# Two more pairs of heads turned on VectorE and through memory instead of by TensorE, in a banded attention with a gated product

## The chip, the core and the metric

The kernel runs on one core of a Trainium2 chip. TensorE (PE) multiplies matrices, VectorE (DVE), ScalarE (ACT) and GpSimd (POOL) work on vectors, and SyncE (SP) issues the transfers between the chip's memory and the on-chip tiles. The metric is the device time of one execution in microseconds. Three runs of the kernel before took 724.47, 725.68 and 729.17 us; the median is 725.68.

## What is computed

The reference is a local attention with global tokens, followed by a gated product of dense layers:

```
k_all, v_all = concat([k_g, k_l]), concat([v_g, v_l])
out_g = softmax(q_g @ k_all.T / 8) @ v_all               # 32 global tokens see everything
s_ll  = where(|i - j| <= 32, q_l @ k_l.T / 8, -1e9)      # 512 local tokens see a band
s_lg  = q_l @ k_g.T / 8                                  # and the global tokens
out_l = softmax(concat([s_lg, s_ll])) @ concat([v_g, v_l])
x     = rows of concat([out_g, out_l])                   # 4608 tokens, 512 wide
out   = ((x @ w1) * (x @ w2)) @ w3 @ w_out               # 1024 wide inside
```

There are 8 batches and 8 heads of width 64.

## The kernel before

**Attention.** Two heads of one batch make a *pair*; the 32 pairs are numbered from 0, four to a batch (`pair`, with `m` the number and `NP` = 4). For each pair TensorE makes the scores (`scores`, 32 instructions in the program, 64 records in the trace), VectorE takes each block's maximum (`minus_max`, eight times), ScalarE the exponentials (`exps`, eight times), and the probabilities have to be turned so that they can stand as weights of the product with the values (`values`). Its result is divided by the sums on VectorE (`normalize`) and has to be turned too, since the dense layers want a token in a column. It is then split into a high and a low part (`convert`, `xh` and `xl`).

**Two ways to turn.** With `m < TP` the probabilities are turned by TensorE: `transposes` makes four 128×128 transposes for each of the two heads into a PSUM bank, and `transposed` copies the bank to the tile `Pt` on ScalarE or VectorE. With `m >= TP`, `turn` turns 32×32 blocks on VectorE (one instruction, the step `tn`), `turned_out` (step `po`) issues four transfers to a tile `Pd` in memory that put the blocks in their places, and `turned_in` (step `pi`) one transfer back to `Pt`. The same holds for the tokens with `XT`: `back` makes four transposes by TensorE into the bank `b`, or `values_turn` (step `vn`), `values_out` (`vw`, four transfers to `vd`) and `values_in` (`vi`, one transfer to `xr`) go by VectorE and memory. Before, `TP` and `XT` are 4: pairs 0 to 3, which are batch 0, go by TensorE, the others by memory. `Pt` and the normalized tile `vo` have one buffer each, `Pd` and `vd` three.

**Weights.** The weights come as 64-bit numbers and are unpacked on ScalarE and VectorE (`fetch` and `unit`, from raw tiles that are used in turn). `w3 @ w_out` is multiplied out first on TensorE, in 64 products of 128×512 (`fold`, two records each), and split (`fold_split`).

**Dense layers.** The tokens are taken in twelve blocks `k`; block 0 holds three quarters of batch 0. For each `k` and each of eight column blocks `m`, `first` makes two products of twelve matmuls (`ap` and `bp`, three for each of the four pairs of the batch), `gate_a`, `gate_b`, `gate_hi` and `gate_lo` multiply and split them, and `second` multiplies with the product of `w3` and `w_out`. The first product of block 0 needs the tokens of pairs 0 to 3.

**The order.** Nothing is scheduled at run time. Every step has a number in the table `ORDER_OF`, and for some a letter that names its engine (A, D or P). `in_order` sorts all steps by these numbers, and they are written to the engines in that sequence, so that each engine's queue, SP's too, is in this order, and an instruction that waits holds up what stands behind it on its engine. `add` gives a step its engines and what it depends on, `take` and `read` what a buffer's reuse depends on.

Of the kernel before, what the change touches and what calls it, by code (L numbers as in the profile page):

```python
# [19 lines left out]
def i(ap):  # L20
# [8 lines left out]
LAG, TP, XT, LATE, VC, VL = 0, 4, 4, 4, 4, 10  # L29
# [15 lines left out]
    load="5 9 2 4 26 3 16 10 45 133 44 60 193 72 200 230 190 310 154 203 291 246 373 301 442 457 404 447 680  "  # L45
# [5 lines left out]
    clear="0 1 8",  # L51
    edges="27",
    warm="17",
    fetch="6 7 21 15 19 24 41 59 55 69 76 79 101 96 107 122 126 142 158 148 162 219 257 255 256 285 304 340 366  "
    "341 369 403 189 216 225 441 488 498 500 519 554 558 584 569 611 642 645 604",
    unit="D22 12 23 D25 29 33 A47 48 56 A42 30 49 A43 52 63 D57 53 64 D67 65 78 D85 91 99 D86 74 87 D100 103  "
# [8 lines left out]
    fold="50 70 81 117 119 141 170 175 58 71 93 118 123 140 167 197 62 94 97 116 127 139 204 209 82 90 98 115  "  # L65
    "145 153 159 164 215 226 234 262 267 283 299 325 270 279 307 332 380 397 413 418 317 324 337 393 398  "
    "439 445 462 345 348 354 360 386 407 423 435",
    w34h="D187 A220 D236 D169 A326 A444 D475 A438",
    w34l="198 250 260 171 338 449 479 455",
    vc="A13 A137 D173 P83 P46 D40 P199 A342 P252 P275 P298 D295 A432 D392 A683 A706 D704 A752 P796 A774 P895  "  # L70
# [4 lines left out]
    vs="P61 A66 P84 D160 A92 A73 P80 D228 A102 P95 P108 P112 A243 P263 D356 A269 P850 A854 D905 A878 D906  "  # L75
# [7 lines left out]
    kc="A11 D14 A20 P28 D77 P113 P106 A165 P224 D265 P306 D311 A472 P478 A516 A486 A634 D615 A649 D667 P764  "  # L83
# [4 lines left out]
    s="18 51 182 239 294 364 485 539 646 711 793 833 915 955 1057 1098 1152 1217 1302 1342 1431 1474 1569  "  # L88
    "1609 1699 1757 1858 1904 1983 2027 2109 2171",
    mm="37 32 34 36 31 38 35 39 178 88 68 149 131 146 105 161 210 227 191 192 195 194 196 212 245 248 259  "  # L90
# [11 lines left out]
    ex="155 111 75 54 130 166 89 134 211 128 180 168 179 152 156 184 237 244 221 214 202 201 233 218 288 253  "  # L102
# [11 lines left out]
    tp="174 181 223 238 251 276 329 344",  # L114
    pt="A176 D183 A229 A241 A264 A280 D330 A358",
    v="188 242 292 370 490 588 687 714 798 858 916 958 1058 1100 1157 1223 1305 1373 1433 1478 1571 1614  "
    "1703 1751 1860 1905 1985 2029 2112 2172 2260 2293",
    iv="172 231 274 346 469 518 625 700 735 822 887 935 982 1072 1106 1198 1249 1331 1383 1472 1561 1600  "
    "1691 1749 1815 1880 1928 2014 2051 2159 2206 2272",
    nm="222 258 343 411 514 596 693 723 807 860 926 963 1068 1103 1173 1235 1325 1376 1447 1492 1577 1623  "  # L120
    "1717 1754 1865 1912 1988 2039 2117 2178 2267 2296",
    xt="254 335 384 421",
# [990 lines left out]
```

## Time and profile before

| What | us |
|---|---|
| median of three runs | 725.68 |
| the profiled execution's own time | 725.34 |
| its span on the core | 723.4 |
| TensorE busy | 708.2 |
| VectorE busy | 452.4 |
| ScalarE busy | 346.5 |
| GpSimd busy | 143.4 |

The profile is of one execution. Busy times are unions of the engine's instructions. A matmul's end is modelled, and consecutive matmuls overlap in the records; the distance from start to start, which the chain of waits shows, is what one costs TensorE. The chain of waits follows the last instruction back to whatever released each step. The DMA share is the mean busy share of the core's 16 DMA engines.

### The profile page before, as it was taken

To read this page: it belongs to the slowest core of one execution; us is meant where nothing else is said; L and a number is where in the kernel's file an instruction comes from. 1 tells how busy PE (TensorE), PEld (TensorE's weight loads), DVE (VectorE), ACT (ScalarE), POOL (GpSimd) and SP (SyncE) were. 2 spreads that over 40 slices of the span, in tenths; PEclk is the share of its full clock that TensorE was granted. 3 is DMA by queue.
4 is the path that set the end of the run, shared out by engine and by line. 5 is a ranking of instruction groups with operands and counts; after the bars stand their busy time and mean duration, and the time that the engine had idled before them with its cause. 6 is when DMAs were issued, how large, how long until landed. Compare 5 with 4: busy or idle time off the path is not lost.

```text
span 723.4 us, 22413 instructions
## 1 busy us (share of the span) xinstructions
PE 708.2 (98%) x9076; PEld 624.3 (86%) x9076; DVE 452.4 (63%) x1367; ACT 346.5 (48%) x931; POOL 143.4 (20%) x200
## 2 busy tenths in 40 slices
PE   5999999999999999999999999999999999999997
PEld 3455589889999999899999999998999999999996
DVE  3689998876867657656756565567857645333222
ACT  4878975855555455673546343454434142001121
POOL 3403231221232333011122132104001121010000
PEclk8899999999999999999999999999999999999999
DMA  8998888898786567557554645656365531111010
GB/s 277 281 296 280 247 238 250 249 260 247 197 233 187 158 186 196 164 153 209 158 182 133 195 145 150 189 159 175 93 184 126 176 89 48 33 44 44 1 31 29
DMA packets 87902, 121.01 MB, mean 167 GB/s; under 512 B 14040, under 2 KB 53336, under 8 KB 87800
## 3 DMA queue, kind: packets, MB, share of 16 engines
q1 hardware_dynamic: 87800, 119.59, 56.8%
q8 instruction: 71, 1.16, 0.7%
q14 instruction: 31, 0.25, 0.1%
HBM read 81.80 MB, written 37.75 MB: 165 GB/s over the span
## 4 chain that ended last, share of the span: by engine, by line
PE 94%; DMA 3%; SPq 1%; DVE 1%; issue 1%; ACT 0%
PE bp L585 8%; PE acc L618 8%; PE ap L585 8%; PE bp L587 8%; PE bp L586 8%; PE w L738 8%; PE acc L619 8%; PE ap L587 8%; PE ap L586 8%; PE acc L620 8%; PE v L425 5%; PE s L373 5%; PE sg L507 2%; PE gx L536 2%; DMA raw_w<-in_w_t_dram 1%; DMA raw_w12s<-in_w_t_dram 1%
## 5 line engine op out<-in xcount | busy, mean ns | idle before, releaser
L385 ACT ACTIVATE P<-P,mn 128x128 f32<-128x128 f32 x256 | 100.8, 395 | 88.0 <-DVE mn L380 71.7
L585 PE MATMUL bp<-x,w12h 128*128 128x384 f32 (+1 forms) x384 | 124.1, 323 | 0.4 <-DVE as__7581 L595 0.4
L585 PE MATMUL ap<-x,w12h 128*128 128x384 f32 (+1 forms) x384 | 123.9, 323 | 0.0
L586 PE MATMUL bp<-x,w12h 128*128 128x384 f32 (+1 forms) x384 | 122.0, 318 | 0.0
L587 PE MATMUL bp<-x,w12l 128*128 128x384 f32 (+1 forms) x384 | 122.0, 318 | 0.0
L586 PE MATMUL ap<-x,w12h 128*128 128x384 f32 (+1 forms) x384 | 122.0, 318 | 0.0
L587 PE MATMUL ap<-x,w12l 128*128 128x384 f32 (+1 forms) x384 | 122.0, 318 | 0.0
L380 DVE CUSTOM_DVE_ANT_0 P<-s,cs 128x128 f32<-128x128 f32 x256 | 63.6, 282 | 36.8 <-PE s L373 34.9
L585 PEld LDWEIGHTS bp<-x,w12h 128*128 128x128 f32 x384 | 72.6, 189 | 2.7 <-DVE as__7581 L595 0.7
L585 PEld LDWEIGHTS ap<-x,w12h 128*128 128x128 f32 x384 | 72.6, 189 | 2.5 <-issue 0.2
L586 PEld LDWEIGHTS ap<-x,w12h 128*128 128x128 f32 x384 | 72.7, 189 | 1.4 <-issue 0.2
L586 PEld LDWEIGHTS bp<-x,w12h 128*128 128x128 f32 x384 | 72.7, 189 | 1.1 <-issue 0.2
L587 PEld LDWEIGHTS ap<-x,w12l 128*128 128x128 f32 x384 | 72.6, 189 | 0.0
L587 PEld LDWEIGHTS bp<-x,w12l 128*128 128x128 f32 x384 | 72.6, 189 | 0.0
L329 POOL COPY V<-V 32x384 f32<-32x384 f32 (+1 forms) x53 | 52.6, 997 | 89.5 <-DMA V<-in_v_t_dram 83.4
L738 PE MATMUL w<-wo,w3f 128*128 128x512 f32 x128 | 61.9, 629 | 8.3 <-DVE wo L652 6.2
L738 PEld LDWEIGHTS w<-wo,w3f 128*128 128x128 f32 x128 | 24.3, 201 | 34.3 <-issue 22.9
L385 ACT ACTIVATION_READ_ACCUMULATOR P<-P,mn 128x1 f32 x256 | 48.5, 190 | 0.0
L329 ACT COPY V<-V 32x1536 f32<-32x1536 f32 (+1 forms) x40 | 45.2, 1136 | 4.0 <-DMA V<-in_v_t_dram 3.3
L393 DVE STREAM_TRANSPOSE P<-P 128x1024 f32<-128x1024 f32 x28 | 34.6, 1236 | 12.6 <-ACT P L385 12.6
L339 ACT COPY V<-vg 32x1024 f32<-32x1024 f32 x35 | 36.6, 1044 | 7.2 <-PE gx L541 6.5
L339 POOL COPY V<-vg 32x1024 f32<-32x1024 f32 x18 | 19.3, 1073 | 99.6 <-PE gx L541 75.3
(1017 smaller groups left out, 1340.7 us busy)
## 6 DMA issues: line engine op xcount, KB each, us to landing
Pd<-P SPq DMA_DIRECT2D x112, 128.0 KB, 3.0
Pt<-Pd SPq DMA_DIRECT2D x28, 512.0 KB, 4.2
raw_w<-in_w_t_dram SPq DMA_DIRECT2D x24, 512.0 KB, 6.2
K<-in_kp_t_dram SPq DMA_DIRECT2D x36, 272.0 KB, 4.2
V<-in_v_t_dram SPq DMA_DIRECT2D x36, 256.0 KB, 4.7
out_dram<-o SPq DMA_DIRECT2D x34, 256.0 KB, 2.6
q<-in_q_t_dram SPq DMA_DIRECT2D x32, 256.0 KB, 3.7
vd<-vo SPq DMA_DIRECT2D x112, 64.0 KB, 3.4
```

Source lines behind the costliest of these rows:

```text
L329: (nc.scalar.copy if eng is nc.scalar else eng.tensor_copy)(to, src)
L339: (nc.scalar.copy if eng is nc.scalar else eng.tensor_copy)(to, src)
L373: nc.tensor.matmul(block(st[:, h], x, 128 * g), q[64 * h : 64 * h + 64, c : c + 32], window(m, h, 4 * g + x), start=True, stop=True, skip_ ...
L380: nc.vector.tensor_tensor_reduce(T["P", m][:, :, h, g], chunks(T["s", m][:, h, 128 * g : 128 * g + 128]), chunks(masks[g]), -0.125, 3.0e38 ...
L385: nc.scalar.activation(P, P, AF.Exp, bias=T["mn", m][:, g, h : h + 1], scale=-1.0, accum_out=T["sm", m][:, g, h : h + 1])
L585: nc.tensor.matmul(d, wh[:, j, c, :], hi, start=(j == 0), stop=False, skip_group_check=True)
L586: nc.tensor.matmul(d, wh[:, j, c, :], lo, start=False, stop=False, skip_group_check=True)
L587: nc.tensor.matmul(d, wl[:, j, c, :], hi, start=False, stop=(j == 3), skip_group_check=True)
L618: nc.tensor.matmul(a, gh[:, sl], wh, start=(m == 0), stop=False)
L619: nc.tensor.matmul(a, gh[:, sl], wl, start=False, stop=False)
L620: nc.tensor.matmul(a, gl[:, sl], wh, start=False, stop=(m == 7))
L738: nc.tensor.matmul(T["w34", t], T["w3f", t, j // 4][:, j % 4], T["wo"][:, j], start=(j == 0), stop=(j == 7))
```

## The change

`TP` and `XT` go from 4 to 2, so pairs 2 and 3 take the way by VectorE and memory for both probabilities and tokens. The tables of `ORDER_OF` are replaced as a whole: every step of the kernel has a new number and many a new engine. No function is changed.

```
-LAG, TP, XT, LATE, VC, VL = 0, 4, 4, 4, 4, 10
+LAG, TP, XT, LATE, VC, VL = 0, 2, 2, 4, 4, 10
...
-    tp="174 181 223 238 251 276 329 344",
-    pt="A176 D183 A229 A241 A264 A280 D330 A358",
+    tp="179 185 223 235",
+    pt="A183 D188 A229 A243",
...
-    tn="419 480 565 662 749 783 852 899 974 1039 1096 1172 1245 1290 1366 1424 1519 1563 1632 1690 1818 1838  "
+    tn="245 293 408 483 594 653 743 793 847 886 1001 1039 1101 1173 1224 1312 1370 1427 1517 1555 1643 1705  "
...
```

The start of TensorE's queue before (`s0` and `s1` are the scores of pairs 0 and 1, `w34` the products of `w3` with `w_out`, `q` and `K` the loaded queries and keys; the last part of a name is a buffer's number):

```order
L915 MATMUL warm_134<-og_74 128x128 x10
L373 MATMUL s0_145<-K0_75,q0_109 32x128 x32
L738 MATMUL w34_0_227<-wo_96,w3f0_0_187 128x512
L373 MATMUL s1_229<-K1_76,q1_132 32x128 x32
L738 MATMUL w34_1_273<-wo_96,w3f1_0_270 128x512
L738 MATMUL w34_2_279<-wo_96,w3f2_0_225 128x512
```

And of the change:

```order
L915 MATMUL warm_130<-og_74 128x128 x10
L373 MATMUL s0_141<-K0_75,q0_114 32x128 x32
L373 MATMUL s1_233<-K1_76,q1_178 32x128 x32
L738 MATMUL w34_0_270<-wo_96,w3f0_0_197 128x512
L738 MATMUL w34_1_279<-wo_96,w3f1_0_221 128x512
L738 MATMUL w34_2_284<-wo_96,w3f2_0_204 128x512
```

The first product stood between the two scores and now stands behind both.

TensorE's queue before, from the scores of pair 5 to the global scores `sg2` (`v3` are the values of pair 3, `xt2` and `xt3` the tokens of pairs 2 and 3 turned by TensorE):

```order
L373 MATMUL s5_904<-K1_76,q5_730 32x128 x32
L425 MATMUL v3_947<-V0_77,Pt3_852 32x64 x32
L738 MATMUL w34_5_698<-wo_96,w3f5_1_622 128x512
L447 MATMUL xt2_997<-cs_73,vo2_873 128x4x32 x4
L738 MATMUL w34_7_880<-wo_96,w3f7_1_901 128x512
L738 MATMUL w34_6_831<-wo_96,w3f6_0_717 128x512
L738 MATMUL w34_5_698<-wo_96,w3f5_1_622 128x512
L738 MATMUL w34_6_831<-wo_96,w3f6_1_725 128x512
L738 MATMUL w34_7_880<-wo_96,w3f7_1_901 128x512
L738 MATMUL w34_5_698<-wo_96,w3f5_1_622 128x512 x2
L447 MATMUL xt3_1043<-cs_73,vo3_1032 128x4x32 x4
L738 MATMUL w34_7_880<-wo_96,w3f7_1_901 128x512
```

And of the change, over the same stretch:

```order
L373 MATMUL s5_898<-K1_76,q5_687 32x128 x32
L425 MATMUL v3_941<-V0_77,Pt3_850 32x64 x32
L738 MATMUL w34_6_760<-wo_96,w3f6_0_696 128x512
L738 MATMUL w34_7_857<-wo_96,w3f7_0_743 128x512
L738 MATMUL w34_6_760<-wo_96,w3f6_1_762 128x512 x2
L738 MATMUL w34_7_857<-wo_96,w3f7_0_743 128x512 x2
L738 MATMUL w34_7_857<-wo_96,w3f7_1_1010 128x512 x3
L738 MATMUL w34_6_760<-wo_96,w3f6_1_762 128x512
L507 MATMUL sg2_1045<-K0_75,qg1_441 32x4x32 x2
```

The token transposes are gone, and ten products stand between the values of pair 3 and the global scores; two more stand between those and the first product of block 0.

SP's queue in the change, from the probabilities of pair 2 to those of pair 3 coming back (`raw` are weights before unpacking; before the change none of the `Pd` and `Pt` rows of pairs 2 and 3 is there):

```order
L400 DMA Pd2_671<-P2_446 32x4x256 x4
L303 DMA q5_687<-in_q_t_dram 128x512
L306 DMA K1_76<-in_kp_t_dram 128x544
L702 DMA raw_w120_0_699<-in_w12_t_dram 128x1024
L406 DMA Pt2_716<-Pd2_671 128x1024
L702 DMA raw_w120_1_722<-in_w12_t_dram 128x1024
L400 DMA Pd3_735<-P3_598 32x4x256 x4
L332 DMA vg_80<-in_vg_t_dram 32x512
L702 DMA raw_w121_1_757<-in_w12_t_dram 128x1024
L303 DMA q6_840<-in_q_t_dram 128x512
L406 DMA Pt3_850<-Pd3_735 128x1024
```

Each trip out and back has other loads between its two halves on this queue. The way of the tokens of pair 3 follows: `vd3` behind the five loads of V for pair 4, then `xr2`, one load of weights and `xr3`.

## Rows read from the trace of the kernel before

**Rows 1.** The page's first part: busy us (share of the span) xinstructions.

```profile
PE 708.2 (98%) x9076; PEld 624.3 (86%) x9076; DVE 452.4 (63%) x1367; ACT 346.5 (48%) x931; POOL 143.4 (20%) x200
```

**Rows 2.** Waits of TensorE, whole run: total us, times, longest us.

```profile
PE w L738 <- DVE wo L652: 6.2, 1, 6.2
...
PE bp L585 <- DVE as__7581 L595: 0.4, 1, 0.4
```

**Rows 3.** A stretch: PE, PEld, DVE, ACT, POOL busy, granted clock, DMA share, GB/s.

```profile
100.00:120.00 20.00, 20.00 (x285) 18.21 (x275) 19.20 (x71) 12.97 (x42) 3.09 (x5) 1.00 0.85 247
```

**Rows 4.** The chain of waits, 40 to 130 us: start us, us, what.

```profile
61.61 0.44 PE t L411 x4
...
76.84 1.09 PE s L373 x64
77.93 1.03 PE v L425 x64
...
80.45 6.01 PE w L738 x14
86.46 0.44 PE xt L447 x4
...
87.76 0.87 PE sg L507 x48
...
91.40 0.16 PE ap L585
...
109.30 0.36 PE ap L585
```

**Rows 5.** Timeline, 0 to 50 us: start, us, engine, line, tiles [idle before, releaser].

```profile
6.52 1.11 SPq L702 DMA_DIRECT2D raw_w<-in_w_t_dram  x2
...
15.33 1.96 PE L373 MATMUL s<-K,q 64*32 64x128 f32 x64
...
19.35 26.24 PE L738 MATMUL w<-wo,w3f 128*128 128x512 f32 x54 [2.06 <-DVE w3f L652]
```

**Rows 6.** TensorE's groups of instructions: xcount, busy us, mean ns, idle before.

```profile
L411 PE MATMUL t<-cs,P 128*128 128x128 f32 x32 | 4.9, 276 | 0.0
```

**Rows 7.** DMA issues of the first 30 us: xcount, KB each, median us to landing.

```profile
K<-in_kp_t_dram SPq DMA_DIRECT2D x4, 272.0 KB, 9.8
```

**Rows 8.** Stretches of 2 us in the head, columns as in rows 3.

```profile
14.00:16.00 2.00, 2.00 (x30) 0.67 (x34) 1.97 (x7) 0.76 (x1) 1.51 (x2) 0.50 1.09 244
...
24.00:26.00 2.00, 2.00 (x4) 0.84 (x4) 0.76 (x2) 1.77 (x2) 1.36 (x2) 0.74 1.05 213
```

**Rows 9.** Timeline of VectorE, 40 to 125 us: the two kinds of turns.

```profile
85.59 1.24 DVE L393 STREAM_TRANSPOSE P<-P 128x1024 f32<-128x1024 f32 x1
...
106.92 0.70 DVE L452 STREAM_TRANSPOSE vo<-vo 128x512 f32<-128x512 f32 x1
```

**Rows 10.** Timeline of SP, 56 to 150 us: pair 4's trips.

```profile
86.86 1.79 SPq L400 DMA_DIRECT2D Pd<-P  x4
...
92.05 0.33 SPq L406 DMA_DIRECT2D Pt<-Pd  x1
...
109.77 1.93 SPq L458 DMA_DIRECT2D vd<-vo  x4
...
115.10 0.33 SPq L462 DMA_DIRECT2D xr<-vd  x1
```

**Rows 11.** DMA issues from 60 to 110 us, columns as in rows 7.

```profile
Pt<-Pd SPq DMA_DIRECT2D x2, 512.0 KB, 6.9
```

**Rows 12.** DMA issues of the whole run, columns as in rows 7.

```profile
Pt<-Pd SPq DMA_DIRECT2D x28, 512.0 KB, 4.2
...
xr<-vd SPq DMA_DIRECT2D x28, 256.0 KB, 3.9
```

**Rows 13.** The page's groups: the exponentials and the reading of their sums.

```profile
L385 ACT ACTIVATE P<-P,mn 128x128 f32<-128x128 f32 x256 | 100.8, 395 | 88.0 <-DVE mn L380 71.7
...
L385 ACT ACTIVATION_READ_ACCUMULATOR P<-P,mn 128x1 f32 x256 | 48.5, 190 | 0.0
```

More of the change, by code (lines that the diff above doesn't have):

```diff
@@ L66 @@
[L66 to L70, printed above, removed]
[4 rows of a table removed]
-    vs="P61 A66 P84 D160 A92 A73 P80 D228 A102 P95 P108 P112 A243 P263 D356 A269 P850 A854 D905 A878 D906  "
[7 rows of a table removed]
-    kc="A11 D14 A20 P28 D77 P113 P106 A165 P224 D265 P306 D311 A472 P478 A516 A486 A634 D615 A649 D667 P764  "
[4 rows of a table removed]
@@ L117 @@
[L117 to L122, printed above, removed]
-    xh="D278 D302 A339 D352 A387 D388 A428 A425 D602 A745 A737 P746 A743 A747 A762 D786 P888 P1012 D920  "
[3 rows of a table removed]
@@ L144 @@
-    gq="470 440 627 618 759 776 866 870 995 996 1136 1140 1257 1265 1381 1379 1525 1520 1643 1645 1795 1791  "
-    "1949 1935 2055 2056 2199 2198 2261 2308 2377 2383",
-    gr="504 643 778 885 1020 1141 1287 1382 1553 1647 1805 1960 2103 2207 2320 2386",
-    ge="507 522 681 689 782 784 898 900 1030 1050 1153 1156 1292 1297 1399 1402 1555 1558 1651 1689 1812  "
-    "1816 1962 1968 2105 2110 2210 2228 2322 2324 2388 2389",
-    gt="524 699 815 913 1090 1168 1303 1416 1568 1693 1846 1990 2158 2232 2332 2391",
@@ L150 @@
-    go="530 710 817 914 1092 1177 1309 1445 1570 1718 1867 1995 2160 2233 2334 2394",
-    gi="639 742 837 943 1107 1200 1329 1465 1586 1734 1895 2020 2168 2281 2343 2401",
-    vg="674 766 869 989 1129 1255 1384 1503 1628 1758 1934 2054 2196 2298 2360 2420",
-    gn="679 789 874 992 1132 1296 1425 1562 1656 1772 1981 2099 2202 2302 2368 2424",
-    gd="861 880 1006 1004 1184 1486 1449 1747 1956 1899 1982 2253 2252 2404 2398 2427",
-    gin="2433 2435 2443 2449",
-    gxh="A2439 P2445 P2454 A2458",
@@ L157 @@
-    gxl="P2440 D2446 P2462 P2459",
-    first="451 466 476 496 521 529 547 572 603 616 628 650 692 678 721 722 769 779 785 804 823 847 859 872 891  "
[9 rows of a table removed]
-    ga="A468 A511 D540 A581 A617 A658 A702 D750 D781 A809 D856 D879 D911 D950 A969 A1014 A1032 A1056 D1085  "
[5 rows of a table removed]
-    gb_="477 517 556 586 632 669 707 751 788 824 862 884 912 953 986 1017 1037 1064 1095 1126 1151 1179 1199  "
[4 rows of a table removed]
-    gh="A489 A535 A567 A606 A647 A675 A725 D757 D790 D826 A867 A894 D934 A957 D988 A1023 A1043 D1076 D1109  "
[5 rows of a table removed]
-    gl="499 536 579 613 652 686 739 758 792 830 871 901 937 965 1000 1026 1049 1080 1111 1137 1167 1182 1208  "
[4 rows of a table removed]
@@ L190 @@
-    second="508 561 595 636 663 701 753 761 814 834 883 907 946 977 1010 1034 1065 1091 1121 1145 1170 1204 1230  "
[4 rows of a table removed]
-    out="A773 D775 A777 D1046 A1051 A1055 A1274 D1278 A1282 A1468 D1469 A1470 A1695 A1696 A1700 A1872 A1882  "
-    "D1889 A2093 D2094 A2108 A2277 D2278 D2290 A2408 A2409 A2411 D2489 A2490 D2496 A2553 A2557 A2609  "
-    "A2612 D2611",
-    store="1008 806 1009 1053 1052 1097 1322 1340 1288 1644 1585 1487 1836 1755 1701 2068 1883 1948 2152 2151  "
-    "2238 2366 2314 2364 2452 2453 2429 2501 2497 2498 2559 2558 2610 2613",
+    load="9 5 6 2 10 3 20 19 27 128 51 48 159 62 199 201 191 361 186 129 264 272 446 322 430 468 487 434 674  "
[5 rows of a table added]
@@ new lines @@
+    clear="0 1 102",
+    edges="26",
+    warm="17",
+    fetch="4 7 11 8 14 33 39 54 66 86 83 93 98 111 123 119 145 155 152 168 169 224 216 230 273 289 332 310 404  "
+    "359 424 435 144 212 221 443 511 513 521 517 553 584 588 571 618 623 658 612",
+    unit="A24 21 29 A32 31 35 A45 46 49 D30 28 34 A58 57 63 D73 64 75 A79 72 82 D87 85 88 A104 103 107 D117  "
[8 rows of a table added]
+    fold="61 84 101 115 148 161 172 176 67 100 113 130 138 209 214 227 71 92 120 142 153 182 196 204 99 108  "
+    "131 136 156 162 167 170 238 256 262 268 274 280 287 295 298 301 308 318 328 343 357 363 312 339 352  "
@@ new lines @@
+    "377 390 395 418 429 335 389 397 402 405 412 415 433",
+    w34h="D180 A282 A233 A173 A304 D365 A437 A442",
+    w34l="189 284 236 175 316 369 439 445",
+    vc="D23 A22 D16 D25 A47 A12 P240 P198 P258 D305 A556 A416 P378 A486 A695 P679 A771 A724 D777 A784 P770  "
[4 rows of a table added]
+    vs="A44 A65 A77 P52 P70 P60 D181 D217 P78 D151 P247 A80 P239 A253 P345 P251 P819 A824 A869 P826 P916  "
[7 rows of a table added]
+    kc="A13 D15 P53 A55 A96 P91 D97 P112 P222 P226 A311 A314 P460 P461 A518 A506 A619 D633 P655 A656 A779  "
[4 rows of a table added]
+    s="18 59 187 244 319 364 470 537 665 699 803 839 897 946 1049 1099 1162 1223 1290 1346 1432 1474 1573  "
@@ new lines @@
+    "1605 1686 1755 1852 1894 1976 2024 2128 2161",
+    mm="43 37 36 41 42 50 38 40 125 127 89 69 74 122 90 68 207 205 215 218 228 194 193 203 263 250 261 275  "
[11 rows of a table added]
+    ex="106 56 76 105 114 81 94 95 126 132 158 210 146 177 166 165 211 231 220 241 242 200 195 232 276 281  "
[11 rows of a table added]
+    tp="179 185 223 235",
+    pt="A183 D188 D229 A243",
+    v="190 248 320 370 495 589 676 716 806 863 900 948 1053 1102 1169 1227 1294 1378 1439 1477 1574 1606  "
+    "1692 1757 1853 1898 1969 2025 2129 2163 2265 2300",
@@ new lines @@
+    iv="124 219 288 344 447 532 646 678 731 828 892 940 1022 1087 1114 1214 1245 1337 1410 1471 1540 1583  "
+    "1662 1730 1810 1885 1920 1990 2076 2154 2256 2297",
+    nm="197 278 329 375 523 600 677 723 818 867 915 955 1065 1112 1177 1232 1306 1383 1447 1487 1582 1621  "
+    "1718 1767 1861 1910 1986 2035 2142 2179 2268 2302",
+    xt="234 294",
+    xh="A249 A237 D317 D306 A421 A464 D432 P488 A624 P748 P666 D749 A739 A760 D772 D817 P1000 D1007 P934  "
[3 rows of a table added]
+    xl="254 283 351 326 D431 D530 D436 D492 P654 P755 P692 D751 D752 D783 D773 P937 D1011 P1015 P935 P1014  "
[3 rows of a table added]
@@ new lines @@
+    tn="245 293 408 483 594 653 743 793 847 886 1001 1039 1101 1173 1224 1312 1370 1427 1517 1555 1643 1705  "
+    "1754 1847 1919 1982 2071 2119 2162 2257",
+    po="252 297 417 490 601 662 756 797 849 890 1005 1046 1104 1179 1228 1313 1373 1429 1520 1568 1649 1716  "
+    "1756 1849 1922 1983 2085 2123 2201 2259",
+    pi="286 330 441 533 638 683 776 821 878 912 1025 1067 1125 1194 1252 1330 1393 1449 1547 1581 1670 1732  "
+    "1844 1862 1941 2000 2104 2136 2240 2269",
+    vn="338 381 531 614 691 728 829 870 918 958 1079 1141 1193 1238 1322 1407 1459 1530 1586 1658 1733 1776  "
@@ new lines @@
+    "1867 1933 1991 2041 2146 2191 2278 2303",
+    vw="342 387 560 630 697 730 834 879 924 959 1081 1144 1202 1247 1333 1411 1462 1531 1590 1701 1744 1778  "
+    "1868 1946 2003 2043 2150 2251 2279 2319",
+    vi="396 409 593 659 720 745 905 911 949 982 1188 1199 1212 1269 1438 1448 1533 1597 1675 1752 1788 1790  "
+    "1959 1965 2052 2137 2270 2272 2316 2336",
+    sg="427 585 759 866 984 1129 1255 1382 1499 1632 1779 1923 2048 2181 2262 2367",
+    gq="456 457 651 590 764 767 888 895 1021 997 1140 1134 1259 1263 1396 1394 1544 1523 1636 1654 1781 1798  "
@@ new lines @@
+    "1935 1940 2063 2091 2190 2184 2276 2299 2375 2369",
+    gr="474 663 785 914 1030 1148 1268 1399 1548 1697 1800 1956 2097 2198 2310 2380",
+    ge="482 499 689 690 790 795 919 931 1041 1073 1150 1163 1270 1273 1400 1402 1553 1559 1712 1713 1813  "
+    "1826 1960 1994 2101 2102 2202 2203 2313 2321 2383 2386",
+    gt="516 701 800 933 1090 1208 1274 1418 1561 1724 1831 1998 2113 2235 2324 2394",
+    go="525 706 809 939 1092 1211 1280 1420 1565 1727 1843 2002 2115 2239 2335 2398",
+    gi="647 738 841 947 1113 1237 1301 1455 1601 1753 1864 2022 2140 2286 2352 2405",
@@ new lines @@
+    vg="667 763 871 989 1132 1258 1386 1494 1633 1780 1924 2050 2183 2307 2368 2423",
+    gn="673 778 875 993 1136 1262 1390 1519 1657 1786 1927 2090 2233 2358 2371 2426",
+    gd="741 971 1028 1013 1142 1458 1515 1702 1717 1832 1953 2287 2293 2376 2374 2428",
+    gin="2434 2439 2448 2454",
+    gxh="A2444 A2449 A2456 P2461",
+    gxl="P2447 P2451 P2458 P2463",
+    first="440 450 458 475 484 512 542 559 570 603 628 635 660 687 725 734 774 780 788 798 830 820 853 874 889  "
[9 rows of a table added]
+    ga="D455 A472 D534 D557 D615 A636 A711 A750 D782 D804 A840 A880 D917 D941 D965 A1002 A1027 A1070 D1094  "
[5 rows of a table added]
@@ new lines @@
+    gb_="459 507 536 577 621 661 732 754 789 811 854 884 926 944 973 1008 1045 1074 1095 1128 1154 1192 1210  "
[4 rows of a table added]
+    gh="D463 A514 A539 A605 A629 A694 D736 A761 D796 A822 A868 A896 A929 D950 D985 A1018 A1050 D1078 A1100  "
[5 rows of a table added]
+    gl="469 520 541 607 632 698 740 762 801 833 876 899 932 963 996 1020 1059 1082 1111 1131 1180 1201 1218  "
[4 rows of a table added]
+    second="505 529 595 616 649 702 747 766 813 843 882 920 943 972 1006 1034 1071 1093 1124 1153 1191 1203 1231  "
[4 rows of a table added]
+    out="D775 D799 D802 A1055 D1056 D1061 D1284 A1286 D1296 A1488 A1489 D1491 A1707 A1708 A1720 D1895 A1896  "
@@ L200 @@
+    "A1897 A2111 D2112 D2114 D2261 D2275 A2277 D2407 D2409 A2410 A2492 D2494 D2496 D2556 A2571 A2611  "
+    "D2613 A2614",
+    store="901 805 930 1068 1197 1069 1355 1354 1372 1490 1585 1638 1721 1719 1765 1958 1996 1901 2197 2188  "
+    "2121 2295 2351 2298 2436 2437 2411 2495 2561 2558 2557 2575 2612 2615",
 )
```

25 lines of the change are left out of this document (removed), and 174 rows, old and new, of tables (ex, first, ga, gb_).

## The prediction

> **What bounds the kernel now.** I read the page's busy line first: TensorE is busy for 708.2 of 723.4 us, and no other engine comes near [rows 1]. A busy TensorE may still be waiting inside its busy time, so the waits come next. Its longest one is 6.2 us for the first unpacked piece of `w_out`, early in the run; the longest past the head is 0.4 [rows 2]. The chain of waits shows the same: from 19.35 us it runs along TensorE piece by piece [rows 4, 5]. So behind the head a microsecond of TensorE work is a microsecond of the kernel, and a wait that a change puts there is one too.
>
> The sum goes against the profiled execution: 725.34 us, which is its span of 723.4 and 1.9 around it. The median of the three timed runs, 725.68, lies 0.3 above. About 1% (7.3 us) is what a measurement of this kernel can tell from no change, so the bounds are 718.4 and 732.9.
>
> **What TensorE loses.** Pairs 2 and 3 give up two groups of four transposes each for the probabilities and one each for the tokens: six groups of four, 24 transposes. A group takes 0.44 us of the chain, for the probabilities as for the tokens [rows 4]. That is 6 × 0.44 = 2.64 us. I take the chain's step, not the record's own length (276 ns, [rows 6]), since records overlap: four would be 1.10 us, and the next group's start says 0.44.
>
> The skill prices this step otherwise. The Trainium skill's page "VectorE: DVE Perf Modes", section "The three transpose paths", gives 390 ns for a 128×128 transpose (bf16) on TensorE; by that, as an estimate, 24 of them are 9.4 us and the time would come out near 717 us. The row (0.11 us each in the chain) decides here.
>
> A second saving is in the order. After a run of small matmuls (scores, values, global ones) the first large one stands 0.36 us in the chain where its like takes 0.16 [rows 4], so each such switch costs 0.20. Counted down both orders there are 56 switches before and 52 after: 0.8 us. Together TensorE has 3.44 us less to do.
>
> **What the new order does to the head.** Before, one product of `w3` with `w_out` stands ahead of pair 1's scores and was done before them; the unbroken chain starts at 19.35 [rows 5]. After, both pairs' scores stand first, and no product is done when they end. That gives back one product: 14 records (seven products) take 6.01 us, so 0.86 each [rows 4].
>
> The scores themselves come later. K and q of pair 1 are the 12th and 13th issues of SP instead of the 8th and 10th. Before, the 12th was out by 7.6 us [rows 5]; K loads of the first 30 us took 9.8 us to land (median, [rows 7]), which makes 17.4; spreading K is one copy, some 0.6; the scores took 1.96 us here, at the half clock [rows 5, 8]. So the chain starts near 20.0 to 20.6, and I take 20.3, 0.95 later than 19.35. The bounds: if K lands as fast as the eighth issue did it is hidden behind the unpacking that holds the start now (2 us earlier at best, when `w3` is ready first); if the 13th issue waits as it does now, a further 3 us. The clock was granted at half (1.2 GHz) from before these scores until within 24 to 26 us, some six us into the chain [rows 8]. Either order has the same kind of products there, so I cost the clock at nothing; if its rise comes 2 us later with the start, that is 1 us more.
>
> So far 725.34 − 3.44 + 0.86 + 0.95 = 723.7 us.
>
> **What is added.** VectorE gets two turns of probabilities (1.24 us each) and two of tokens (0.70) [rows 9], 3.9 us, less a copy. SP gets 2 × (4 + 1 + 4 + 1) = 20 issues, some 0.4 us each [rows 10]. The queue moves, by the tiles' shapes, 2 × (512 + 512 + 256 + 256) KB = 3.1 MB more. ScalarE is relieved. VectorE was busy for 19.20 of 20 us from 100 to 120, the DMA engines for 0.85 [rows 3], so none of that is free by itself; what hides it is the TensorE work between a turn and its reader.
>
> *Probabilities of pair 2.* The turn stands on VectorE right ahead of the first minus-max of pair 3, so about where scores 3 end. TensorE then has values 1 (1.03), 12 products (10.3), one token group (0.44) and scores 4 (1.09) before values 2: 12.9 us of cover. The nearest trip is pair 4's before: first piece out at 86.86, back out at 92.05 [rows 10], landing 6.9 us later [rows 11], 12.1 in all, plus the turn 1.24: 13.3. With the whole run's median landing of 4.2 [rows 12] it is 10.7. So a wait of 0 to 0.4, and more if the turn is late.
>
> *Pair 3.* From scores 3 to values 3 there are 21.0 us of the same pieces. The exponentials take eight times 0.395 + 0.190 us [rows 13], 4.7, and about as much ScalarE work stands between them; say 8.5 until the turn. 12.5 of cover for 10.7 to 13.3: a wait of 0 to 0.8. Its way back waits for values 2 as well, since there is one Pt buffer.
>
> *Tokens of pair 3.* Here the cover is thinnest. After values 3 come 10 products, the global scores (0.87), 2 products, and the nine matmuls of the first product of k = 0 that don't need pair 3: 8.6 + 0.87 + 1.7 + 1.5 = 12.7. Against it: normalize 0.7, turn 0.70, then as before from 109.77 to 115.10 for the way out [rows 10], landing 3.9 [rows 12], about 0.9 for hi and lo: 11.5. Before, the turned tokens also sat from 107.6 to 109.77 behind another issue of SP [rows 9, 10], which makes 13.7. In the new order SP has the loads of V for pair 4 just ahead of them. So 0 to 1.0. Behind SP's wait for the tokens stand the weights of `w12` for m = 2 and 3, wanted some 10 us later.
>
> These waits don't add in full, because one that has passed gives the next trip its time. I take 1.0 for the three (0 to 2.2). All later stages are in a new order too; the longest wait past the head is 0.4 us now [rows 2], and I add 0.5 (0 to 3). The last stage is the same in both: eighteen matmuls behind the last a-product, nothing to gain.
>
> 723.7 + 1.5 = **725.2 us**: what the transposes free is given back at the start and at the first product.
>
> **The rivals.**
>
> *A clean saving.* All trips hidden, and the chain starts 0.86 earlier, which pays for the product that is not yet done: 725.34 − 3.44 = 721.9. For it: the trips' shorter ends all fit their covers, and K of pair 1 may land in less than 9.8. Against it: the 12th issue.
>
> *Slower: the queue is late with everything before the first product.* 3.1 MB at the 247 GB/s of 100:120 [rows 3] are 12.7 us of queue; if nothing could be put off, 723.7 + 12.7 = 736.4. It decides (over 732.9) from 9.2 us of waits on. Against it, the order puts off V of later pairs: by the shapes, 25.4 MB are queued up to the tokens of pair 3, against 24.3 MB ahead of pair 4's probabilities, which went out at 86.86 [rows 10]. The excess of 1.1 MB is 4.5 us, so 728 to 729 is this rival's nearer form. The Trainium skill speaks for this side: "VectorE: DVE Perf Modes", section "Rules for kernel authors", sends a full 128×128 transpose to TensorE where the result may lie in PSUM, and here it may.
>
> *VectorE becomes the bound* from 60 to 120 us: its 3.9 us come out whole, 723.7 + 3.9 = 727.6. For it 19.20 of 20; against it, the planner's order moves V and K copies to POOL and ScalarE there.
>
> *The records' length is the price:* 24 × 0.276 = 6.6 [rows 6], 725.34 − 6.6 − 0.8 + 1.8 = 719.7, with no wait. The skill's figure above is the far end of this rival and shares its chance; against both stands the chain's 0.44 for four.
>
> **How the numbers follow.** The forecast 0.58, the clean saving 0.17, the late queue 0.12 (0.04 of it over 732.9), VectorE 0.08, the records 0.03, something else 0.02. The likeliest case alone spans 723 to 728. The clean saving, less a little for an earlier start, puts the low end at 721.5, and the queue's nearer form with a late head the high end at 730; what is left out is under 2 in 10. Faster than 718.4 needs the records' price and an early start together: 0.02. Slower than 732.9: 0.05 with an unforeseen stall. Within 1%: 0.93.
>
> **What would show it.** No transposes after pair 1 and 52 switches; the chain's start near 20.3; a wait of TensorE for Pt or for x of pair 3 below 1.5 us each; the first product of k = 0 near 91 to 93 us against 91.40 [rows 4]; the DMA share from 40 to 100 at 0.85 or more. Wrong would be: TensorE waiting over 3 us at values 2, values 3 or the first product; a chain that starts before 19 or after 22; or a new wait after 130 us of over 2 us.

## The result and the profile after

| | median of the runs, us | ratio to the kernel before, 95% interval |
|---|---|---|
| before | 725.89 | |
| after | 737.49 | 1.0144 (1.012 to 1.0167) |

The change makes the kernel 1.4% slower, 10.5 us by the ratio. The forecast was 725.2, the range 721.5 to 730. The profiled execution of after took 738.03 us, its span is 736.2 against 723.4.

The page of after, busy us of each engine and packets, MB and share of the DMA queues:

```profile
PE 708.4 (96%) x9052; PEld 624.0 (85%) x9052; DVE 470.8 (64%) x1391; ACT 346.0 (47%) x927; POOL 128.1 (17%) x180
...
q1 hardware_dynamic: 90680, 122.74, 57.8%
q8 instruction: 71, 1.16, 0.7%
```

TensorE has 24 matmuls fewer than in [rows 1], and yet is busy as long; the time between its work has grown by 12.6 us. The last row will matter: 71 packets of 16 KB that hold instructions. The waits of TensorE, whole run:

```profile
PE s L373 <- DMA q<-in_q_t_dram: 11.3, 2, 8.4
PE v L425 <- issue: 5.4, 2, 4.2
PE ap L585 <- DVE as__1649 L465: 1.3, 1, 1.3
PE gx L536 <- DMA Gt<-Gd: 1.1, 1, 1.1
PE warm L915 <- POOL K L273: 1.0, 1, 1.0
PE v L425 <- PE gx L541: 0.9, 1, 0.9
```

The first row is the head, which before had other waits, the longest of 6.2 us [rows 2]; the row of `warm` was there before too. The second is new, and so are the other small ones: before, no wait past the head was over 0.4. None of them is for Pt or for x of pair 3. The largest is in the middle of values 1 (TensorE's timeline, 54 to 64 us):

```profile
55.12 1.16 PE L373 MATMUL s<-K,q 64*32 64x128 f32 x64
56.21 0.91 PE L425 MATMUL v<-V,Pt 128*32 128x64 f32 x49
61.29 0.65 PE L425 MATMUL v<-V,Pt 128*32 128x64 f32 x15 [4.17 <-issue]
```

49 of the group's 64 records are done, then nothing happens for 4.17 us, and no semaphore ends it: "issue" means that the profile shows nothing that was waited for. Its consequences are in the chain of waits, where 12 matmul records behind the gap (a product is two) take 7.50 us and the next 12 take 5.15:

```profile
61.94 7.50 PE w L738 x12
...
69.87 5.15 PE w L738 x12
```

and in the stretches of 10 us (PE, PEld, DVE, ACT, POOL busy, granted clock, DMA share, GB/s):

```profile
60.00:70.00 10.00, 8.71 (x32) 4.17 (x33) 5.98 (x15) 5.40 (x19) 0.00 (x0) 0.69 0.90 280
70.00:80.00 10.00, 10.00 (x147) 5.17 (x146) 5.80 (x22) 5.25 (x12) 0.75 (x2) 1.00 0.44 125
```

Behind the gap the granted clock was at half (1.2 GHz; 0.50 in the row of 60 to 66 us, a mean of 0.69 over these 10), and that costs 2.35 us more, 7.50 less 5.15. The DMA share of 0.44 is a third consequence: SP stood still for scores 4, which came late, and everything queued behind it (SP's waits, 50 to 100 us):

```profile
SPq L303 <- PE s L373: 7.0, 1, 7.0
```

The second new place is the stretch in which scores, values and global work of pairs 5 to 10 lie between the first products. 5.15 us of 50 are idle in it, 0.36 in the kernel before (the row of after, then that of before):

```profile
130.00:180.00 50.00, 44.85 (x731) 40.34 (x730) 39.23 (x130) 30.76 (x86) 10.36 (x14) 0.97 0.89 241
130.00:180.00 50.00, 49.64 (x915) 43.91 (x914) 37.10 (x131) 30.65 (x96) 11.13 (x14) 1.00 0.87 250
```

From 180 to 300 us it is 1.12 against 0.00.

### The profile page after: what moved, and what is told of

It reads as the page before. It is cut to its first block, busy times and chain, and to the rows that moved or that the text cites. A ratio compares the mean times of both kernels' runs of the same rounds, so it can differ in the third digit from the quotient of the medians.

```text
span 736.2 us, 22374 instructions
## 1 busy us (share of the span) xinstructions
PE 708.4 (96%) x9052; PEld 624.0 (85%) x9052; DVE 470.8 (64%) x1391; ACT 346.0 (47%) x927; POOL 128.1 (17%) x180
## 4 chain that ended last, share of the span: by engine, by line
PE 81%; DMA 8%; ACT 5%; DVE 3%; issue 2%; SPq 1%; POOL 0%; ACTq 0%; DVEq 0%
PE bp L585 7%; PE acc L618 7%; PE ap L585 7%; PE acc L620 7%; PE bp L586 7%; PE bp L587 7%; PE ap L587 7%; PE ap L586 7%; PE acc L619 7%; PE w L738 4%; PE v L425 4%; PE s L373 4%; DMA raw_w12s<-in_w_t_dram 2%; DMA raw_wo<-in_wo_t_dram 2%; PE sg L507 2%
## 5 line engine op out<-in xcount | busy, mean ns | idle before, releaser
L329 POOL COPY V<-V 32x384 f32<-32x384 f32 (+1 forms) x42 | 43.2, 1031 | 99.6 <-DMA V<-in_v_t_dram 95.3
L329 ACT COPY V<-V 32x1536 f32<-32x1536 f32 (+1 forms) x54 | 53.1, 991 | 5.0 <-DMA V<-in_v_t_dram 4.0
L339 POOL COPY V<-vg 32x1024 f32<-32x1024 f32 x23 | 24.5, 1065 | 177.7 <-PE gx L541 146.1
L373 PE MATMUL s<-K,q 64*32 64x128 f32 x2048 | 38.6, 283 | 11.8 <-DMA q<-in_q_t_dram 11.3
L373 PEld LDWEIGHTS s<-K,q 64*32 64x32 f32 x2048 | 29.7, 109 | 21.5 <-issue 10.0
```

The lines of the kernel that those rows point to most:

```text
L329: (nc.scalar.copy if eng is nc.scalar else eng.tensor_copy)(to, src)
L373: nc.tensor.matmul(block(st[:, h], x, 128 * g), q[64 * h : 64 * h + 64, c : c + 32], window(m, h, 4 * g + x), start=True, stop=True, skip_ ...
```

## The experiments

Three theories. **A, late code:** the gap is TensorE out of instructions. **B, traffic:** the 3.1 MB push the later loads back. **C, order:** the re-solved order has waits of its own, whatever it moves.

**Moving the packets' borders.** A *border* is the place in TensorE's stream where one packet of instructions ends and the next begins. For A speaks where the gap lies. I counted TensorE's records in the trace (weight loads, matmuls, semaphore instructions, by start): the gap is behind record 961. 71 packets for 18,244 records are one for every 257, 256 if a record is 64 bytes (71 times 16 KB over 18,244 records is 63.8), and the page of the kernel with 256 more of them (N = 64 below) has 72. And no packet of q8 arrived from 53 to 58 us, though the queue was busy throughout (DMA packets by queue, 53:58 and 58:60):

```profile
q1 hardware_dynamic: 540, 1.62, 100.7%
...
q1 hardware_dynamic: 555, 0.72, 102.2%
q8 instruction: 1, 0.02, 2.9%
```

That packet starts at 58.91 and ends at 59.85, 1.4 us before TensorE resumes; its own 0.94 us are no more than other packets take (a median of 1.0), so it was late before it started. SP had queued four loads, 1.8 MB, shortly before the gap (SP's timeline, 48 to 70 us):

```profile
51.48 0.33 SPq L702 DMA_DIRECT2D raw_w<-in_w_t_dram  x1
51.90 0.38 SPq L702 DMA_DIRECT2D raw_w12s<-in_w_t_dram  x1
52.33 0.90 SPq L702 DMA_DIRECT2D raw_w<-in_w_t_dram  x2
```

If TensorE waited for this packet, instructions put in ahead of the gap move the borders, and 256 of them move nothing. The edit, where N matmuls of one column are 4 N instructions:

```diff
+        for _ in range(N * (m == 0)): nc.tensor.matmul(T["z"][0:32, 0:1], og[:, 0:32], og[:, 0:1], start=True, stop=True)
...
-        z = ps_acc.tile([128, 512], F32, tag="acc", name="warm")
+        z = T["z"] = ps_acc.tile([128, 512], F32, tag="acc", name="warm")
```

N = 32, in the kernel after:

> The changed kernel with 32 matmuls of one column (128 of TensorE's instructions) issued right behind scores 0, into a buffer that nobody reads, in the 8.4 us in which TensorE waits there for q of pair 1. Nothing else differs. Late code (theory A: the 4.17 us gap in the middle of values 1 at 57.12 us is TensorE out of instructions, because the 16 KB packet of its instruction queue that lands at 58.96 to 59.95 was asked for when the queue held 1.8 MB of loads): the 128 instructions move the place at which that packet is asked for ahead of these loads, so the gap is gone, scores 4 starts near 68.5 instead of 75.0, the queue's wait for it (7.0 us at 76.16) falls below 1 us, the DMA share of 70 to 80 us rises from 0.44 to over 0.8, the waits of 130 to 175 us shrink, and the time is 724 to 730 us. Traffic (theory B: the 3.1 MB that the turned pairs move push all later loads back): 735 to 738 us, since the bytes are the same. Order (theory C: the new order of the table costs by itself): 735 to 738 us.

Measured: 736.66 us, ratio 1.0143 (1.0084 to 1.0201), profiled execution 735.15. The gap is gone, SP no longer waits for scores 4, and clock and DMA share of 60 to 80 us are up again, as A says:

```profile
60.00:70.00 10.00, 10.00 (x58) 4.63 (x58) 8.75 (x27) 9.19 (x28) 0.00 (x0) 1.00 0.87 288
70.00:80.00 10.00, 10.00 (x256) 5.79 (x239) 8.77 (x37) 5.43 (x15) 1.44 (x3) 1.00 0.91 288
```

But the time hardly moved, where A had forecast 724 to 730. A part of the reason is on TensorE's timeline: there are new stops of the same kind, four of 0.5 to 1.2 us, 3.2 together, against the 6.5 that gap and clock had cost. The rest is not placed; the interval, from four runs, leaves room for a gain of 0.6%. Two of the stops:

```profile
104.29 1.09 PE L425 MATMUL v<-V,Pt 128*32 128x64 f32 x61
105.91 0.30 PE L425 MATMUL v<-V,Pt 128*32 128x64 f32 x3 [0.54 <-issue]
...
146.18 0.86 PE L425 MATMUL v<-V,Pt 128*32 128x64 f32 x45
148.23 0.53 PE L425 MATMUL v<-V,Pt 128*32 128x64 f32 x19 [1.19 <-issue]
```

N = 64:

> The same with 64 such matmuls, 256 instructions, which is what one 16 KB packet holds at 64 bytes each, so the packets' borders fall on the same places of the program as in the changed kernel. Theory A: the gap of about 4 us in values 1 is back, and the time is 734 to 739 us, although this kernel differs from the one with 128 by 32 matmuls in idle time alone. If the gain of the other came from a warmer TensorE or from a later start of the products, this one has it too: 724 to 730 us. Theories B and C: 735 to 738 us for both.

Measured: 738.45, 1.0148 (1.0114 to 1.0181). The gap is back, in the same place of the program, with 256 more records ahead of it:

```profile
PE v L425 <- issue: 3.4, 1, 3.4
```

N = 15. By the trace of after, 60 instructions leave no border just ahead of a burst of scores and values, which run 256 records in 2.2 us.

> The changed kernel with these 15 idle matmuls and all of its bytes. With 128 instructions the gap of values 1 went and four stalls of 0.7 to 1.4 us at other borders came; at 60 the borders leave bursts of 2.2 us alone almost everywhere. A: no stall over 0.5 us at a border outside the head, profile 4 to 6 us shorter than the changed kernel's, time 730 to 734 us. If late packets cost nothing in the end (B alone): 736 to 738 us.

Measured: 733.04, 1.0066 (1.0039 to 1.0093). One stop of 1.4 us was left (at 191.9), which I had not expected; the rest is as A says. Fifteen matmuls that compute nothing give back 0.78%, 5.7 us; the intervals of the two ratios do not overlap.

Three controls, the same edit in the kernel before:

> The kernel before with the same 32 idle matmuls behind scores 0. A control on the inserted instructions: where no packet of instructions is late they should neither help nor hurt by more than 1.5 us (theory A for the changed kernel alone); if they gained some 3 us here too, their effect there would be the clock's or the head's and not the packet's.

> The kernel before with 64 idle matmuls (256 instructions: the borders where they were). With 32 it was 0.57 per cent slower, and its profile had stalls of 2.0 and 1.3 us that ended 1.4 us behind the landing of a packet of instructions. A: no such stall, within 1.5 us of the kernel before (0.998 to 1.002). If the inserted matmuls themselves cost the time, twice as many cost at least as much: 1.005 or more.

> The kernel before with the same 15 idle matmuls. A control for the kernel with 15: by the places of the packets' borders no stall here either, so within 1.5 us of the kernel before (0.998 to 1.002). If the 15 matmuls gained by the clock of the head, it would be faster by 3 us or more, as the changed kernel was by 5.

Measured with N = 32: 730.63, 1.0057 (1.0034 to 1.008); N = 64: 728.58, 1.0012 (0.998 to 1.0045); N = 15: 729.31, 1.0005 (0.9973 to 1.0038). So the matmuls don't help by themselves, and 32 of them hurt, which I had not expected, where 64 don't. The larger of the two stops that they bring with N = 32:

```profile
97.46 1.08 PE L425 MATMUL v<-V,Pt 128*32 128x64 f32 x59
100.32 0.31 PE L425 MATMUL v<-V,Pt 128*32 128x64 f32 x5 [1.78 <-issue]
```

With N = 64 there was one stop of 1.2 us against what I expected, at the border of values 1, and no difference in time that could be measured. The places of the stops of 0.5 us or more of idle time that cut a group of equal matmuls in two and have no releaser, past the head and over all kernels of this study, settle A:

| kernel | start of the stops, us (records ahead of them) |
|---|---|
| before | none |
| after | 57.1 (961) |
| after, N = 64 | 57.9 (961 + 256) |
| after, N = 32 | 105.4 (961 + 5 × 256), 147.0 (961 + 10 × 256), 185.0 (961 + 15 × 256), 316.9 (961 + 31 × 256) |
| after, N = 15 | 191.9 (961 + 16 × 256) |
| after, a quarter of the bytes (below) | 56.5 (961) |
| after, TensorE's transposes put back (below) | 56.6 (961) |
| new order, then old, N = 32 (below) | 381.3 (961 + 38 × 256) |
| before, N = 32 | 98.5 (961 + 5 × 256), 416.0 (961 + 43 × 256) |
| before, N = 64 | 56.6 (961 + 256) |
| the other seven kernels | none |

All thirteen lie on one grid of 256 records, and they end 1.3 to 1.6 us after a packet of instructions has landed. The other borders say the same: at 1,161 of them, from record 961 on in all 17 kernels, the first record behind the border never starts sooner than 1.27 us after its packet has landed. That the loads make a packet late is read from the queue alone; no run takes the four loads away.

**What the bytes cost.** First the bytes without the change: the third and fourth pair's tiles written and read back by nobody, in the kernel before.

```diff
...
+        if m in EXTRA:
+            take("Pd", 3, ("Pe", m), ("eo", m))
+            add(("eo", m), "SP", ex, extra_out, "P", m)
+            read(("eo", m), ("P", m))
+            add(("ei", m), "SP", [("eo", m)], extra_in, "P", m)
...
```

> The kernel before, with what the third and fourth pair would move through memory added and used by nobody: their probabilities and tokens are written as the other pairs' are (16 transfers of 128 or 64 KB) and read back in 4 transfers of 512 or 256 KB (into memory again, as the cores' own memory is full). TensorE's order and instructions are those of before. It is the price of the 3.1 MB alone. Theory B: 731 to 738 us, with waits of TensorE for weights between 95 and 175 us. Theory A: 725 to 729 us, waits below 3 us in sum.

Measured: 739.07, 1.0163 (1.0128 to 1.0197). That reads like B, even above its range, and TensorE's waits (46 to 140 us) begin with

```profile
PE xt L448 <- DVE x L480: 3.3, 1, 3.3
PE ap L597 <- ACT as__1188 L477: 2.3, 1, 2.3
PE bp L597 <- DVE x L480: 1.7, 1, 1.7
```

But I had put the transfers into SP's order by hand, and SP waited 5.2 us for the way back alone, with all loads behind it. It shows that the transfers don't go into the old order for nothing, not what the bytes cost in the new one. So the other way round: the kernel after with a quarter of them.

```diff
-        for x in range(4):
+        for x in range(1 if kind == "P" and m < 4 else 4):
...
+        d = d[:, 0:256] if kind == "P" and m < 4 else d
...
-        for x in range(4):
+        for x in range(1 if m < 4 else 4):
...
+        n = 128 if m < 4 else 512
...
```

> The changed kernel with its new order, its turns on VectorE and TensorE's instructions as they are, but with a quarter of the third and fourth pair's traffic: one of the four transfers that write each tile, and a read of that quarter (these pairs' output is left wrong: values and tokens use the quarter that is there for the rest). 0.8 MB instead of 3.1 MB, 12 queue issues fewer. Late code (A) alone: the gap of 4 us in values 1 lies ahead of the first of these transfers' effect and stays, time 735 to 738 us. Traffic (B: the bytes are what the later waits pay for): the gap stays, the waits of 110 to 300 us fall by half or more, 730 to 734 us. Order (C: the new order's own places of scores, values and middle products): waits of 130 to 190 us stay near 5 us, 734 to 738 us.

> The same with 15 idle matmuls (60 instructions) behind scores 0, which by the places of the packets' borders (every 256th instruction) leave no border ahead of a burst of scores and values while the queue is full. A and B together: no gap, short waits, 724 to 729 us. C: 729 to 733 us.

Measured: 736.59, 1.0127 (1.0087 to 1.0167), against 1.0144 with all the bytes; with N = 15, 732.68, 1.0072 (1.0044 to 1.01), against 1.0066. The gap of values 1 is in the first and not in the second. Three quarters of the bytes and 12 issues of SP are worth nothing that these runs can tell. B falls, for the new order: with a quarter of the bytes the gap is still 4.17 us, and the idle time from 130 to 180 us 4.77 (5.15 with all the bytes).

**What the order costs.** The new order with TensorE's transposes back in it (their 24 put behind values 1 to 3):

```diff
-LAG, TP, XT, LATE, VC, VL = 0, 2, 2, 4, 4, 10
+LAG, TP, XT, LATE, VC, VL = 0, 4, 4, 4, 4, 10
...
```

> The new table of ranks, but with probabilities and tokens of the third and fourth pair turned by TensorE as before (their 24 transposes put behind values 1, values 2 and values 3, where TensorE has products to do), so without the 3.1 MB. Theory A: the gap in values 1 lies ahead of everything that differs and stays at about 4 us, the queue's wait for scores 4 stays near 6 us; the time is 733 to 741 us. Theory B: without the bytes it is back to 725 to 730 us. Theory C: 735 to 741 us, as A; A and C differ in the gap and in the runs with instructions put in.

Measured: 740.08, 1.017 (1.0136 to 1.0204), with a stop of 3.6 us at record 961 and without the bytes. As a price of the order it is too high: the table was solved for other steps, and SP waited here for buffers that TensorE freed late (SP's waits, 55 to 100 us):

```profile
SPq L702 <- DVE w3f L652: 16.1, 3, 8.6
SPq L702 <- DVE w12l L468: 8.5, 2, 8.1
```

Cleaner are kernels that take one order up to a step and the other from there on. Only the table is edited for this; the idle matmuls and the quarter of the bytes that some of them have are the edits above.

> The kernel before up to the first w12 product, TensorE's transposes and all, and from there on the new order. No added bytes, no gap in values 1. Theory C: waits of 4 to 6 us between the first product and 185 us, 729 to 733 us. Theory B: as the kernel before, 724 to 728 us.

> The changed kernel with the 32 idle matmuls behind scores 0 (which the run with 128 instructions showed to take the gap in values 1 away), its new order up to the first w12 product, and from there on the order of the kernel before; the turned pairs and their 3.1 MB all lie in the first part. Order (theory C: the waits of TensorE between 130 and 190 us, about 5 us in the changed kernel, come from where the new order puts scores, values and the middle products there: back to back, each waiting for what the one ahead sets off): these waits fall to the 1 to 2 us of the kernel before, and the time is 727 to 732 us. Traffic (theory B: the loads of that stretch are late because of the 3.1 MB): the waits stay at 4 to 6 us, 733 to 738 us.

> A quarter of the third and fourth pair's traffic (these pairs' output is left wrong), 15 idle matmuls against late packets, the new order up to the first w12 product and the order of the kernel before from there on: the kernel that joined the two orders at this place, with less traffic and 15 instead of 32 idle matmuls. There TensorE waited 9.9 us at 94 us for ScalarE, which waited for weights. If that wait is the price of the 3.1 MB (the weights' transfers stand behind them in the queue; theory B, in the old order): it falls below 4 us here, the waits of 130 to 300 us stay under 2 us, and the time is 723 to 728 us. If it is only that the two orders don't fit together (theory C): it stays at 8 to 10 us and the time is 731 to 736 us.

> The changed kernel with the 15 idle matmuls and all its bytes, its new order up to the first product of the second block of tokens (about 165 us), and the order of the kernel before from there on, where the queue has caught up. Theory C: the waits between 130 and 165 us stay (3 us in the kernel with 15 idle matmuls), those of 180 to 300 us (4.3 us there) fall under 1.5 us; 729 to 732 us against 733. If the later waits are those of late data whatever the order, 732 to 735 us.

The kernel before with the new order behind the first product: 728.35, 1.0018 (0.9987 to 1.005), between the forecasts of B and C. New up to there, old behind it: 738.98, 1.0181 (1.0133 to 1.0228), with one wait of 9.9 us at the seam (waits of TensorE, 45 to 300 us),

```profile
PE ap L585 <- ACT as__1193 L465: 9.9, 1, 9.9
```

which a quarter of the bytes leaves at 8.6, in 739.77, 1.0162 (1.0075 to 1.025):

```profile
PE ap L589 <- ACT as__1164 L467: 8.6, 1, 8.6
```

So the seam is the two orders' misfit and not the bytes; a seam that went with the bytes would have been B's last case. The old order from 165 us on only: 733.59, 1.0077 (1.005 to 1.0104), no better than N = 15 alone. The idle time from 180 to 300 us does fall, from 3.61 to 0.03, but that of 130 to 180 rises from 3.11 to 5.88. The times of these four are blurred by their seams. What they tell apart is the stretch of 130 to 180 us, by the order that runs in it, over all kernels (50 less TensorE's busy time in this stretch, a row of each profile):

| order in 130 to 180 us | kernels | idle, us |
|---|---|---|
| new | after 5.15; N = 32 4.16; N = 64 4.85; N = 15 3.11; TensorE's transposes 5.59; quarter of the bytes 4.77, with N = 15 3.04; old, then new 3.99; old from 165 us on 5.88 | 3.0 to 5.9 |
| old | before 0.36; N = 32 1.52; N = 64 1.30; N = 15 0.86; bytes added 0.95; new, then old 0.83, with a quarter of the bytes 0.85; transposes left out 1.40 | 0.4 to 1.5 |

Neither the bytes nor the transposes nor the packets move a kernel from one group to the other; the order does. The stretches are of time, and hold somewhat different work; counted by work it comes out the same. From the first product to scores 10, less what the matmuls there cost at the chain's steps (an estimate: 0.163 us for each of the first products, 0.217 of the second, 0.85 to 1.1 for a group of scores or values), 3.2 us are left in the kernel before and 8.8 in after; 3.2 to 4.5 in the four kernels with the old order and no stop, seam or added bytes there, 6.6 to 9.9 in those with the new one. What the order does is to be read in the waits of the kernel with the old order first and the new one behind (45 to 300 us):

```profile
PE gx L536 <- DMA Gt<-Gd: 1.5, 2, 1.3
PE v L425 <- PE gx L541: 0.9, 1, 0.9
PE bp L585 <- DVE as__1998 L595: 0.8, 1, 0.8
PE s L373 <- DMA V<-in_v_t_dram: 0.6, 1, 0.6
```

The new order has scores 8, the global values of the third pair of pairs and values 6 back to back; the old one has a first and a second product between the first two of these and a first product between the last two. So the global values wait for Gt, and values 6 wait until VectorE has emptied the one buffer that both use (the row names the group ahead; VectorE's last read of it ends at 136.7 us, values 6 start at 136.78). These two rows are 2.4 of the 3.99 us; the other rows are waits for VectorE, for V and for ScalarE. The means of the table are 4.5 and 1.0: C is worth some 3.5 us of waits.

**What the transposes give back.** The kernel before without the 16 transposes of these probabilities:

```diff
...
-        for g in range(4):
+        for g in range(4 * (m < 2)):
             nc.tensor.transpose(t[:, g], T["P", m][:, :, h, g].rearrange("p s j -> p (s j)"), ident)
...
```

> The kernel before without the 16 transposes of the third and fourth pair's probabilities and with nothing in their place (the copies behind them read the unturned probabilities, so the output of these pairs is left wrong): what TensorE gets back if the rest is free. By the terms of the prediction 4 groups at 0.44 and 3 switches at 0.20 us: 2.2 to 2.4 us less than the kernel before. If the time TensorE gets back turns into waits, or the switch is worth nothing: 0 to 1.8 us less.

Measured: 728.02, 1.0018 (0.9991 to 1.0045). A gain of 0.3% is outside the interval. The waits of the profile past the head, 45 to 300 us, show what became of it; the kernel before has a single one there, of 0.2:

```profile
PE v L426 <- DMA Pt<-Pd: 1.1, 1, 1.1
PE ap L586 <- ACT as__3182 L466: 1.0, 1, 1.0
PE v L426 <- DMA Pd<-P: 0.8, 1, 0.8
```

TensorE comes sooner to data that do not.

## Why the prediction was wrong

**What held.** The start: the first product was forecast near 20.3 and came at 20.45 (TensorE's timeline, 5 to 25 us).

```profile
18.56 1.96 PE L373 MATMUL s<-K,q 64*32 64x128 f32 x64 [8.42 <-DMA q<-in_q_t_dram]
20.45 3.52 PE L738 MATMUL w<-wo,w3f 128*128 128x512 f32 x6
```

What came last, by this row, was not K, from which 20.3 was reckoned, but q, the 13th issue; that the two come out alike is luck. The clock, costed at nothing there, gave time back: it was full from 22 us on (the row of after, then that of before, which had 0.74 still in 24 to 26 [rows 8]).

```profile
22.00:24.00 2.00, 1.97 (x5) 0.57 (x3) 2.00 (x6) 1.69 (x3) 1.07 (x1) 1.00 1.08 269
22.00:24.00 2.00, 2.00 (x4) 0.89 (x3) 1.13 (x4) 1.82 (x2) 0.16 (x1) 0.50 1.04 313
```

The first transposes start at 44.4 against 45.6, but with 52 records of products ahead of them instead of 56. Four records are 1.7 us, so at the same work the head lost 0.5 us, where the forecast had 1.8. The added trips: I allowed 1.0 us for waits at values 2, values 3 and the first product, and there is none of over 0.3. VectorE is busy 18 us longer, where 3.9 were reckoned, and still the longest wait of TensorE for it past the head is 1.3.

**What failed.** Three terms of the sum.

*The later stages, "0.5 (0 to 3)".* They were sized by the longest wait of the kernel before [rows 2], which says nothing about an order that has not run. This term measured 4.8 us in 130 to 180 us and 1.1 behind it. The new order puts its groups there side by side, and I had looked at its rows only up to the first product. The sign that I named (a new wait of over 2 us after 130) would have missed it too: no single wait there is over 1.5.

*The gap in values 1* has no term at all, and is the larger part: 4.17 us, 2.35 for the clock behind it; 5.7 by the run that takes it away. Because of it the first product came at 96.7 (90.8 in the kernel before by the same timeline), where 91 to 93 was forecast. My sign looked at values 2 and 3, and not at values 1. I took TensorE's stream as limited by data and engines, and what was behind each wait was in the order; that the stream itself is loaded, by transfers beside those of the data, is in no row that I had read. Rows for it are on the page, q8 with its packets. Of the kernel before I can now say that no border with a stop lay in its way.

*The saving of 3.44 us* was taken as time of the kernel because the chain runs along TensorE [rows 4]. Left out by itself, two thirds of it (16 transposes and three switches) came to nothing (a time of -0.1 to +0.45%). A chain without slack is no proof that the next piece's data are ready earlier.

The rival of the late queue gave 736.4, close to what came, and for the wrong reason: its price was that of the bytes, and a quarter of the bytes costs the same. The same holds for the rule named beside it, the Trainium skill's "VectorE: DVE Perf Modes", section "Rules for kernel authors", which sends full transposes to TensorE: the time went its way, but no run here shows VectorE's turns or their traffic as the cause.

**The sum now,** in the profiled executions: span +12.8. The gap and its clock 6.5, the stretch of 130 to 180 us 4.8, 180 to 300 us 1.1: 12.4. Against that stand the transposes' 2.6, so about 3 us are placed nowhere; the granted clock of 0.83 from 140 to 150 us (a mean of 0.97 in the row of 130 to 180) is some 1.7 of them, the head 0.5. The places agree: by the timelines after is 5.9 us behind at the first product (96.7 against 90.8) and 12.4 at scores 10 (172.0 against 159.6), and from there to the end the two take the same, 564.2 and 563.8. Open is also a wait of 1.3 us at 173 us, ahead of values 8, which has no releaser and lies off the grid. By the measured ratios: 0.78% for the packets, 0.66% for the rest, of which the order's waits are shown as waits, and as time in the profiles up to scores 10, but not in the time of the whole run: the kernel with the new order behind the first product alone was 0.18% slower, -0.13 to 0.5%, and 3.5 us would be 0.48%. No kernel tried was faster than the one before.

## What to carry to other kernels

A re-solved order is a change of its own: read it to its end, and cost every place where two groups that share a buffer have come to stand side by side. Work taken off the busiest engine is time only where what it does next is ready sooner. And before a gap is put down to data, look whether it cuts a group of equal instructions in two and whether its place in the engine's stream is a multiple of the packet.

## What the runs showed of the hardware

TensorE's instructions come in packets of 16 KB, in a queue beside the data's, and now and then it stands still for one: 71 packets in the page of after, stops of 0.5 to 4.2 us on a grid of 256 records, each ending 1.3 to 1.6 us after a packet landed, and no border passed sooner than that in any kernel. The Trainium skill's page "Runtime: NRT & Kernel Launch", section "Instruction fetch mechanics", says that instructions are fetched in blocks of 16 KiB, 256 instructions each, over a DMA queue that the sequencer drives itself, and that the cost of a border is mostly hidden. The trace agrees with the block, and with the hiding at all but a few of the borders; where a burst of small matmuls met a late packet, one border cost 4.17 us. When a packet is asked for, no row shows; reckoned from the border before it, packets landed 2.1 us later in the median of the first 35 and 7.8 in the gap of after, where the data's queue was busy throughout.

The granted clock fell behind such stops, and behind shorter waits too. In after it was 0.50 from 60 to 66 us, behind the stop of 4.17 us, and 0.50 from 145 to 148 us, behind waits of 1.15 and 0.89 us at 141.6 and 143.6; in the kernel before with N = 32 it was 0.50 from 102 to 104 us, behind the stop of 1.78 us. The kernel after with N = 32, which had no stop there, kept 1.00 from 60 to 70 us.
